# One rank for each operation in a fused set-attention and expert kernel: a new fixed order, a second pass over the PSUM banks, and a reworked start

## The chip, the cores and the metric

The kernel runs on one core of a Trainium2 chip. Five engines work side by side: TensorE (PE in the profile, its weight loads PEld), VectorE (DVE), ScalarE (ACT), GpSimd (POOL), and SyncE (SP), which here only issues DMAs. The metric is the device time of one execution in microseconds (us); the median of several runs is compared.

## The reference, cut to what matters

```
x [4, 12480, 128], inducing I [32, 128], w_in [128, 2048], w_out [2048, 128]
mab(q, kv): s = q @ kv.T / sqrt(128); a = softmax(s); return a @ kv
h   = mab(I, x)                 # 32 rows for each of the 4 batches: the summary
y   = mab(x, h)                 # 49920 rows of 128
g   = relu-like(y @ w_in):  h >= 1: h;  h <= -1: 0;  between: (h + 1)^2 / 4
out = g @ w_out
```

The weights arrive as 8-byte floats and are turned into 4-byte floats on the chip, in pieces of 256 columns.

## The kernel before, in words

A batch is cut into 25 chunks of rows (15 of 512, 10 of 480), and the chunks into seven groups of up to four. For each batch `summarize` makes the summary `h`: the chunks of x are loaded (`xn`) and turned (`xT`), scored against `I`, exponentiated with the group's own maximum (`score`), turned back and multiplied with x (`gather`), which leaves one 128x128 piece `hs[:, g]` and one sum per group. A chain of small steps, `c1` to `c12`, then finds the common maximum, rescales the seven pieces by factors `ff` and adds them up by 14 matmuls in PSUM (`c11`: seven products in two instructions each). `attend` takes the second attention of a group, and its result `aT` is spread by DMA. Since `h @ w_in` is multiplied out once per batch (`multiply`, `spread` into `hw`), the hidden layer of a chunk is one product of `aT` and `hw`.

`chunk(b, c)` does the expert layer: for each of eight steps `k` there are two hidden tiles of 128 rows. Each is a matmul into one of seven PSUM banks (pool `h`; the eighth bank collects the output); `rise` (ScalarE) makes relu(h + 1) from the bank into `w`, `square` (ScalarE) squares both tiles in place, and `bound` (VectorE) takes min(w, max(h, 1)), reading the bank again, after which the bank is free. In six of eight steps `w` is then split into an upper part `hi` (on VectorE, ScalarE or GpSimd) and the rest `lo` (GpSimd), and three matmuls per tile are added to the output, otherwise two passes of full precision.

The two tiles of a step can lie in neighbouring banks. Then one `rise` or one `bound` reads both banks at once; else there are two instructions. The profile shows the joined form as 128x1024 (or 128x960), the single one as 128x512 (or 128x480).

The order of all instructions is fixed before the launch. Every operation is entered by `add` with its engine, cost, lag and a due time; `Plan.order` is a small list scheduler that steps through time, takes for each free engine the ready operation with the lowest due time, and gives out buffers (`Slot`s of the pools in `SLOTS`) as it goes. Due times come from the table `DUE` and, for some 850 operations, from a correction in `SHIFT`. Bank numbers are chosen as an operation is placed (`pick`), near the twin's bank where that is free, and two twins are joined only if they lie next to each other then. The resulting list is emitted as it stands, so each engine works through a fixed queue.

At the start the first batch's x, the weights and the masks are all prepared at once. w_out is loaded through buffers of the pools `w`, `hi` and `lo`, which 16 of batch 0's 25 chunks of x use too (`FIRST`). Matmuls on the identity (`keep_on`, L1184) fill TensorE's gaps from 14 us on.

Of the kernel before, what the change touches and what calls it, by code (L numbers as in the profile page):

```python
# [27 lines left out]
STEP = 1950  # L28

# [5 lines left out]
DUE = {  # L35
# [17 lines left out]
    "end": [-203620],  # L53
# [15 lines left out]
}  # L69

# [100 lines left out]
    },  # L171
}

WARM = (14000, 200)

LONE = {"r": 7750, "t": 3200}

KEEP = 100

WAIT = 175250  # L180

# [3 lines left out]
R = (18, 0.4167)  # L185


class Slot:


    def __init__(self, pool, turn=None, near=None):
        self.pool, self.left, self.until, self.place, self.tile = pool, 0, 0, None, None
        self.turn, self.near, self.pair = turn, near, near is not None
        if near:
            near.pair = True
# [1044 lines left out]
```

## Time and profile before

| | |
|---|---|
| median of 3 runs | 1708.54 us (1708.45 to 1711.73) |
| the profiled execution | span 1712.0 us |
| busy: TensorE / VectorE / ScalarE / GpSimd | 1690.1 / 1633.7 / 1638.5 / 1621.4 us |
| first hidden matmul | 64.69 us after the start of the span |
| moved by DMA | 105.66 MB |

The profiled execution is one execution taken by the hardware profiler, 3.5 us above the median of the runs. A span in which an engine works on an instruction counts as busy; instructions of one engine can overlap a little, and matmul records overlap a lot.

### The profile page before, as it was taken

Reading aid. Unit: us, or ns where it says so; the run is one execution under the profiler, and the core shown is the slowest. Engines: PE = TensorE matmul, PEld = TensorE weight load, DVE = VectorE, ACT = ScalarE, POOL = GpSimd, SP = SyncE. Lnnn points to the kernel's source line nnn. Section 1 sums busy time; section 2 is a strip of 40 time slices with the busy share of each in tenths; the row PEclk is TensorE's granted clock in tenths of the full one; section 3 lists DMA queues with packets and bytes.
Section 4 is the critical chain, followed back from the end, with each engine's and each line's share of the span. In section 5 each row is a group of like instructions: output and inputs, shape, how many; then the busy total and the mean of one; then the engine's idle time right before and its main releaser. Section 6 shows DMA issues by size and latency. Waiting matters only on the chain.

```text
span 1712.0 us, 25022 instructions
## 1 busy us (share of the span) xinstructions
PE 1690.1 (99%) x7716; PEld 1192.6 (70%) x7716; DVE 1633.7 (95%) x2119; ACT 1638.5 (96%) x2380; POOL 1621.4 (95%) x856
## 2 busy tenths in 40 slices
PE   7999999999999999999999999999999999999998
PEld 5756766677766667677776676667777766667776
DVE  5799999999899999999999999999999999999997
ACT  6699999999999999999999999999999999999997
POOL 2599999999999999999999999999999999999998
PEclk9899999999999999999999999999999999999999
DMA  9334433332343233333243333322212111111111
GB/s 275 87 54 81 79 61 65 54 75 50 66 79 74 48 72 66 59 59 70 50 96 54 74 66 69 60 56 55 41 31 58 30 33 36 28 36 36 33 32 18
DMA packets 427095, 105.66 MB, mean 62 GB/s; under 512 B 369842, under 2 KB 412434, under 8 KB 426962
## 3 DMA queue, kind: packets, MB, share of 16 engines
q1 hardware_dynamic: 425874, 103.82, 30.0%
q8 instruction: 61, 1.00, 0.3%
q14 instruction: 72, 0.59, 0.1%
q10 hardware_dynamic: 1088, 0.25, 0.1%
HBM read 48.94 MB, written 25.56 MB: 44 GB/s over the span
## 4 chain that ended last, share of the span: by engine, by line
PE 87%; DVE 6%; ACT 4%; issue 1%; DMA 1%; POOL 0%; SPq 0%; DVEq 0%; ACTq 0%; POOLq 0%
PE banks L1155 61%; PE banks L1083 19%; DVE w L1096 3%; ACT w L1091 2%; ACT w L1077 2%; DVE hi L1122 1%; PE banks L741 1%; PE banks L682 1%; PE banks L896 1%; PE banks L1184 1%; PE banks L725 1%; DMA w<-in_moe_w_out 1%; PE banks L639 1%; DVE oT L1167 1%; PE banks L824 0%
## 5 line engine op out<-in xcount | busy, mean ns | idle before, releaser
L1127 POOL TENSOR_TENSOR lo<-w,hi 128x1024 fp32r<-128x1024 f32 (+1 forms) x599 | 1394.1, 2360 | 20.4 <-PE banks L1155 5.2
L1096 DVE SCALAR_TENSOR_TENSOR w<-banks,w 128x512 f32<-128x512 f32 (+3 forms) x1159 | 953.2, 861 | 22.9 <-ACT w L1077 19.6
L1091 ACT ACTIVATE w<-banks 128x512 f32<-128x512 f32 (+3 forms) x1312 | 832.4, 704 | 22.7 <-PE banks L1083 20.1
L1077 ACT ACTIVATE w<-w 128x1024 f32<-128x1024 f32 (+1 forms) x800 | 826.9, 1068 | 3.1
L1083 PE MATMUL banks<-aT,hw 128*128 128x512 f32 (+1 forms) x1600 | 574.4, 429 | 3.0 <-DVE w L1096 2.1
L1155 PE MATMUL banks<-hi,w_lo 128*128 128x512 f32 (+1 forms) x1198 | 489.5, 409 | 2.9 <-DVE oT L1167 1.5
L1122 DVE TENSOR_REDUCE hi<-w 128x1024 fp32r<-128x1024 f32 (+1 forms) x406 | 474.0, 1176 | 10.8 <-PE banks L1155 1.5
L1155 PE MATMUL banks<-hi,w_hi 128*128 128x512 f32 (+1 forms) x1198 | 464.8, 388 | 0.0
L1155 PE MATMUL banks<-lo,w_hi 128*128 128x512 f32 (+1 forms) x1198 | 410.5, 428 | 0.1
L1083 PEld LDWEIGHTS banks<-aT,hw 128*128 128x128 f32 x1600 | 294.4, 188 | 151.5 <-DVE w L1096 58.8
L1155 PE MATMUL banks<-w,w_f 128*128 128x512 f32 (+1 forms) x804 | 392.1, 582 | 0.0
L1155 PEld LDWEIGHTS banks<-lo,w_hi 128*128 128x128 f32 x1198 | 222.8, 188 | 104.4 <-issue 52.5
L1155 PEld LDWEIGHTS banks<-hi,w_lo 128*128 128x128 f32 x1198 | 225.3, 188 | 83.6 <-issue 17.7
L1155 PEld LDWEIGHTS banks<-hi,w_hi 128*128 128x128 f32 x1198 | 225.5, 188 | 48.9 <-issue 9.9
L1155 PEld LDWEIGHTS banks<-w,w_f 128*128 128x128 f32 x804 | 151.0, 189 | 61.2 <-issue 37.8
L1116 POOL TENSOR_SCALAR hi<-w 128x1024 fp32r<-128x1024 f32 (+1 forms) x145 | 150.1, 1039 | 5.4 <-ACT s L916 0.8
L1167 DVE STREAM_TRANSPOSE oT<-banks 128x512 f32<-128x512 f32 (+1 forms) x100 | 69.3, 693 | 6.7 <-PE banks L1155 6.0
L660 DVE STREAM_TRANSPOSE xT<-xr 128x512 f32<-128x512 f32 (+1 forms) x75 | 50.7, 678 | 2.2 <-DMA xr<-in_x 2.2
L1120 ACT CAST hi<-w 128x1024 fp32r<-128x1024 f32 (+1 forms) x48 | 50.1, 1045 | 1.2 <-DVE w L1096 1.2
L939 POOL TENSOR_TENSOR a<-a,ahi 128x512 fp32r<-128x512 f32 (+3 forms) x28 | 35.7, 1276 | 2.1 <-ACT ahi L936 2.0
L568 POOL TENSOR_TENSOR w_in_sb<-aT,s 128x256 f32<-128x256 f32 x8 | 6.0, 752 | 31.9 <-DVE aT L557 31.9
L682 PE MATMUL banks<-xT,indT 128*32 128x512 f32 (+1 forms) x200 | 30.5, 612 | 0.0
(113 smaller groups left out, 574.6 us busy)
## 6 DMA issues: line engine op xcount, KB each, us to landing
out<-oT SPq DMA_DIRECT2D x240, 64.0 KB, 2.2
xn<-in_x SPq DMA_DIRECT2D x54, 256.0 KB, 4.1
xr<-in_x SPq DMA_DIRECT2D x180, 64.0 KB, 2.8
out<-oT SPq DMA_DIRECT2D x158, 60.0 KB, 2.2
aT<-ahi SPq DMA_DIRECT2D x118, 64.0 KB, 2.0
aT<-a SPq DMA_DIRECT2D x118, 64.0 KB, 2.0
xn<-in_x SPq DMA_DIRECT2D x30, 240.0 KB, 4.2
xr<-in_x SPq DMA_DIRECT2D x120, 60.0 KB, 2.6
```

Source lines behind the costliest of these rows:

```text
L660: nc.vector.transpose(make(xT[b, c])[:, : CW[c]], xr.tile[:, : NB[c]].rearrange("c n i -> c (n i)"))
L682: nc.tensor.matmul(p[q * M : (q + 1) * M, :cw], indT, xT[b, c].tile[:, :cw], start=True, stop=True)
L1077: nc.scalar.activation(w.tile[:, :, :cw], w.tile[:, :, :cw], AF.Square, scale=0.5)
L1083: nc.tensor.matmul(make(h)[:, :cw], hw[b][ft // 4].tile[:, ft % 4 * P : (ft % 4 + 1) * P], aT[b, c].tile[:, :cw], start=True, stop=True,)
L1091: each(of, i, hs_, lambda h, to: nc.scalar.activation(to, h, AF.Relu, bias=1.0), cw, w)
L1096: lambda h, t: nc.vector.scalar_tensor_tensor(t, h, 1.0, t, op0=ALU.max, op1=ALU.min), cw, w,
L1116: nc.gpsimd.tensor_scalar(make(hi)[:, :, :cw], w.tile[:, :, :cw], 1.0, 0.0, op0=ALU.mult, op1=ALU.add)
L1120: nc.scalar.copy(make(hi)[:, :, :cw], w.tile[:, :, :cw])
L1122: nc.vector.tensor_reduce(make(hi)[:, :, :cw], w.tile[:, :, :cw].unsqueeze(3), axis=AX.X, op=ALU.max)
L1127: nc.gpsimd.tensor_sub(make(lo)[:, :, :cw], w.tile[:, :, :cw], hi.tile[:, :, :cw].bitcast(F32))
L1155: nc.tensor.matmul(acc.tile[:, :cw], wt[k][:, i, :], g.tile[:, i, :cw], start=first, stop=(acc.parts == 0),)
L1167: nc.vector.transpose(make(oT)[:, :nb].rearrange("c n i -> c (n i)"), acc.tile[:, :cw])
```

## The change

- Each operation has its own rank in a list `ORDER` of 12093 numbers (the 250 identity matmuls have none, and come last), in place of `DUE`, `SHIFT`, `LONE`, `KEEP` and `WAIT`. The scheduler takes the ready operation of the lowest rank, and holds an engine for one of lower rank that becomes ready before the other would end.
- Where an operation can run on several engines, a string `ON` says on which (599 of its letters are for `hi`).
- Twins are joined whenever both are ready at once, wherever their banks are. After the order is made, `settle` gives out the bank numbers anew by a search that keeps up to 600 partial solutions and counts how many joined pairs are not neighbours; such a pair is issued as two instructions.
- The group sum moves from TensorE to VectorE: seven multiply-adds of 128x128 in `gathered`, then one matmul by `share`. `c3` also repeats the row of maxima, so that `c4` is one matmul.
- Start: the load of `inducing` goes out on ScalarE's DMA queue, and so do seven of batch 0's 16 `spread` transfers instead of two; the clear of `hs` and the masks move to GpSimd; the clamp of a weight block can run on GpSimd; w_out goes through `xr`, `hw` and `oT`; batch 1's loads may not start before 54 us; batch 0's exponentials use three buffers in turn; identity matmuls may start at 1.5 us; the first group's `attend` leaves out its first chunk, which `attend_first` has done.

```diff
-DUE = {
-    "h": [-67510, -9340, -84010, -9090, -128650, -5400, -235200, -125680],
...
-SHIFT = {
...
-WARM = (14000, 200)
-LONE = {"r": 7750, "t": 3200}
-KEEP = 100
-WAIT = 175250
+ORDER = [
...
+ON = (
...
+BEAM = 600
+WARM = (1500, 250)
...
+            choice = {e: w for e, w in choice.items() if e[0] == ON[self.chosen]}
...
+        rank = ORDER[n] if n < len(ORDER) and ORDER[n] >= 0 else 10**9 + n
...
-                    if op.merged and op.beside() and not (op.twin in able[e] and op.twin.ready(e) <= now):
-                        due += op.lone
-                    could.append((due, op.index, op))
+                    could.append((op.rank, op.index, op))
...
-                soon = min((at for due, at in coming if due + WAIT < best[0]), default=math.inf)
+                soon = min((at for rank, at in coming if rank < best[0]), default=math.inf)
...
-                        s.place = s.pick(spare[s.pool], now)
+                        s.place, s.begin = min(i for t, i in spare[s.pool] if t <= now), now
...
-                if best.merged and best.beside():
+                if best.merged and best.placed():
...
+                        x, y = best.uses[0], other.uses[0]
+                        x.mate, y.mate, x.joins, y.joins = y, x, x.joins + 1, y.joins + 1
...
+def settle(done, pool):
+    slots = sorted(dict.fromkeys(s for op in done for s in op.uses if s.pool == pool), key=lambda s: s.begin)
+    ways = [(0, (None,) * SLOTS[pool], None)]
+    for s in slots:
+        found = {}
+        for cost, held, past in ways:
+            held = tuple(x if x and x.until > s.begin else None for x in held)
+            for i, x in enumerate(held):
+                if x:
+                    continue
+                apart = s.mate in held and abs(held.index(s.mate) - i) != 1 if s.mate else False
+                way = cost + s.joins * apart, held[:i] + (s,) + held[i + 1 :], (i, past)
+                if way[1] not in found or way[0] < found[way[1]][0]:
+                    found[way[1]] = way
+        ways = heapq.nsmallest(BEAM, found.values(), key=lambda w: w[0])
+    past = ways[0][2]
+    for s in reversed(slots):
+        s.place, past = past
...
-        nc.vector.memset(hs, 0.0)
-        nc.vector.memset(m, 0.0)
+        nc.gpsimd.memset(m, 0.0)
...
-    ind_in = add("SP", 620, 2000, 100 * EARLY, lambda: nc.sync.dma_start(ind_sb, inducing))
-    masked = add("DVE", 900, 1050, EARLY + 2, masks, [folded], [mask])
+    ind_in = add("ACT", 640, 3000, lambda: nc.scalar.dma_start(ind_sb, inducing), span=(700, math.inf))
+    cleared = add("POOL", 900, 1050, lambda: nc.gpsimd.memset(hs, 0.0))
+    masked = add("POOL", 2400, 2550, masks, [folded], [mask])
...
+        v = single = add(dict(DVE=(268, 400), POOL=(420, 550)), 0, 0, to_single, [v], [home])
...
-        made, f = load_f32(src, when, due, after=got_all[0, 16])
+        made, f, value = load_f32(src, pools=("xr" if k % 2 else "hw", "oT", "oT"))
...
+        later = (54000 if b == 1 else 700, math.inf)
...
-            p1, e1[g] = Slot("h"), Slot("e1")
+            p1, e1[g] = Slot("h"), in_turn("e1") if b or g % 3 == 0 else Slot(["hx", "hy"][g % 3 - 1])
...
-                nc.tensor.matmul(p[:, :M], hs[:, g, :], ff[:, g, :], start=(g == 0), stop=(g == NG - 1))
+        def c10():
+            nc.scalar.activation(share, fold[:, 0, :], AF.Copy, scale=rs)
+        def gathered(groups):
+            a = s_a.tile or make(s_a)
+            for g in groups:
+                to, by = whole if g == NG - 1 else a[:, :C], fr[:, g : g + 1]
+                if g == 0:
+                    nc.vector.tensor_scalar(to, hs[:, g, :], by, None, op0=ALU.mult)
+                else:
+                    nc.vector.scalar_tensor_tensor(to, hs[:, g, :], by, a[:, :C], op0=ALU.mult, op1=ALU.add)
+        def c11():
+            nc.tensor.matmul(make(s_h)[:, :M], whole, share, start=True, stop=True)
...
-        cs = GROUPS[g]
+        cs = GROUPS[g] if b or g else GROUPS[g][1:]
...
-        if of[i].wide:
-            a, b = sorted(h.place for h in hs_)
+        a, b = sorted(h.place for h in hs_)
+        if of[i].wide and b - a == 1:
             do(banks[:, a : b + 1, :cw], *(w.tile[:, :, :cw] for w in ws))
+            return
+        for j in (0, 1) if of[i].wide else (i,):
+            do(hs_[j].tile[:, :cw], *(w.tile[:, half(j, hs_), :cw] for w in ws))
...
     done = plan.order()
+    settle(done, "h")
```

## Rows read from the trace of the kernel before

**Rows 1.** The page's engine shares: busy us, share of the span, instructions.

```profile
PE 1690.1 (99%) x7716; PEld 1192.6 (70%) x7716; DVE 1633.7 (95%) x2119; ACT 1638.5 (96%) x2380; POOL 1621.4 (95%) x856
```

**Rows 2.** Windows by stage: length, busy PE, PEld, DVE, ACT, POOL, clock, DMA share, GB/s.

```profile
0.00:64.69 64.69, 54.25 (x534) 39.36 (x534) 39.52 (x123) 34.44 (x83) 14.53 (x25) 0.92 0.69 209
64.69:1400.00 1335.31, 1330.43 (x5978) 935.11 (x5979) 1294.70 (x1639) 1305.87 (x1880) 1304.92 (x682) 1.00 0.32 62
1400.00:1700.00 300.00, 298.91 (x1186) 214.27 (x1184) 297.51 (x356) 297.77 (x419) 297.58 (x149) 1.00 0.17 32
```

**Rows 3.** The chain that ended last, first 125 us: start us, us, what.

```profile
30.76 5.62 DMA w<-in_moe_w_out
...
42.15 4.73 DMA w<-in_moe_w_out
...
51.47 3.13 PE banks L824 x14
...
64.69 1.12 PE banks L1083 x4
```

**Rows 4.** Order of time: DMA issues of SP, and TensorE's last transposes of x.

```profile
31.43 0.33 SPq L630 DMA_DIRECT2D w<-in_x  x1
34.34 5.05 SPq L630 DMA_DIRECT2D xn<-in_x  x7
...
39.85 0.63 PE L639 MATMUL banks<-ident,w 96*128 96x96 f32 x5
```

**Rows 5.** Windows of the start; the last number is GB/s.

```profile
10.00:20.00 10.00, 9.18 (x49) 6.34 (x47) 6.04 (x16) 6.05 (x12) 2.75 (x4) 1.00 1.05 352
30.00:40.00 10.00, 9.50 (x119) 5.77 (x118) 6.13 (x16) 9.03 (x25) 3.65 (x5) 1.00 1.01 282
```

**Rows 6.** Groups by line: busy us, mean ns | idle us before, releasers.

```profile
L1083 PEld LDWEIGHTS banks<-aT,hw 128*128 128x128 f32 x1600 | 294.4, 188 | 151.5 <-DVE w L1096 58.8 <-issue 29.3 <-DVE banks L902 2.6
...
L1096 DVE SCALAR_TENSOR_TENSOR w<-banks,w 128x512 f32<-128x512 f32 (+3 forms) x1159 | 953.2, 861 | 22.9 <-ACT w L1077 19.6 <-issue 0.2
L1091 ACT ACTIVATE w<-banks 128x512 f32<-128x512 f32 (+3 forms) x1312 | 832.4, 704 | 22.7 <-PE banks L1083 20.1 <-issue 0.2
...
L1122 DVE TENSOR_REDUCE hi<-w 128x1024 fp32r<-128x1024 f32 (+1 forms) x406 | 474.0, 1176 | 10.8 <-PE banks L1155 1.5 <-POOL lo L1127 0.4
...
L1116 POOL TENSOR_SCALAR hi<-w 128x1024 fp32r<-128x1024 f32 (+1 forms) x145 | 150.1, 1039 | 5.4 <-ACT s L916 0.8 <-DVE w L1096 0.7 <-PE banks L1083 0.6
...
L1120 ACT CAST hi<-w 128x1024 fp32r<-128x1024 f32 (+1 forms) x48 | 50.1, 1045 | 1.2 <-DVE w L1096 1.2
...
L824 PE MATMUL banks<-ff,hs 128*128 128x32 f32 x56 | 8.6, 302 | 0.0
```

**Rows 7.** The same view, shapes apart: single and joined, 512-column chunks.

```profile
L1091 ACT ACTIVATE w<-banks 128x512 f32<-128x512 f32 x636 | 357.5, 625 | 11.6 <-PE banks L1083 10.6 <-issue 0.2
...
L1096 DVE SCALAR_TENSOR_TENSOR w<-banks,w 128x1024 f32<-128x1024 f32 x249 | 297.8, 1211 | 9.3 <-ACT w L1077 8.7
...
L1096 DVE SCALAR_TENSOR_TENSOR w<-banks,w 128x512 f32<-128x512 f32 x462 | 292.8, 676 | 3.4 <-ACT w L1077 2.3 <-issue 0.2
...
L1091 ACT ACTIVATE w<-banks 128x1024 f32<-128x1024 f32 x162 | 167.3, 1047 | 0.0
```

**Rows 8.** One line's instructions, a w_out step: ns min/median/max, first to last start.

```profile
L557 DVE SCALAR_TENSOR_TENSOR hi<-w,hi x8: 402/418/426, 29.4 to 72.4; 128x256 f32<-128x256 uint32 x8
```

**Rows 9.** Order of time on VectorE at the start: a step of 128x128.

```profile
57.22 0.28 DVE L1002 TENSOR_TENSOR s<-banks,mx_first 128x128 f32<-128x128 f32 x1
```

**Rows 10.** Order of time on ScalarE: start us, us, merged instructions.

```profile
918.45 1.12 ACT L1091 ACTIVATE w<-banks 128x512 f32<-128x512 f32 x2
919.41 1.11 ACT L1077 ACTIVATE w<-w 128x1024 f32<-128x1024 f32 x1
...
922.00 1.93 ACT L1091 ACTIVATE w<-banks 128x1024 f32<-128x1024 f32 x2
923.81 1.06 ACT L1077 ACTIVATE w<-w 128x1024 f32<-128x1024 f32 x1
```

More of the change, by code (lines that the diff above doesn't have):

```diff
@@ L1 @@
+import heapq
 import math
@@ L408, in o_cols, with took @@
         return out[b * N + OFF[c] : b * N + OFF[c] + CW[c]].rearrange("(i n) c -> i n c", i=M)
-    def begins(b, c):
-        return (b * N + OFF[c]) * NP * STEP // 480
     def cost(c, fixed, each):
         return round(fixed + each * CW[c])
+    def took(w, fixed, each):
+        return round(fixed + each * w)
     FORM = dict(
@@ L506, in attn_moe, with load_f32 @@
     WS = 2 * P
[L508 to L510 removed]
+    def load_f32(src, dst=None, after=None, pools=("w", "hi", "lo")):
+        raw, home = Slot(pools[0]), Slot(pools[1])
+        other = home if pools[1] == pools[2] else Slot(pools[2])
+        mag, top = {}, {}
         rows = src.shape[1]
@@ L520, in take @@
                     nc.vector.tensor_copy(dst, raw.tile.rearrange("p (a b) -> p a b", a=dst.shape[1]))
-            f = add("SP", 700, 3000, when, fetch, [after], [raw])
-            return add("DVE", 205, 335, due, take, [f], [raw]), raw
+                mag[0] = raw.tile
+            f = add("SP", 700, 3000, fetch, [after], [raw])
+            return add("DVE", 205, 335, take, [f], [raw]), raw, mag
         def fetch():
@@ L576, in load_f32 @@
-        v = add("DVE", 420, 550, due, lower, [v], [raw, mag])
+                add_to(dst, by(mag[0]), by(t))
+        f = add("SP", 680, 3000, fetch, [after], [raw], span=(700, math.inf))
+        v = add("ACT", 290, 430, rebias, [f], [home, raw])
+        v = single = add(dict(DVE=(268, 400), POOL=(420, 550)), 0, 0, to_single, [v], [home])
+        v = add("DVE", 270, 400, shift, [v], [home, other])
+        v = add("DVE", 418, 550, upper, [v], [raw, other])
+        v = add("DVE", 263, 395, weight, [v], [home, other])
@@ L577, in load_f32, with load_in @@
+        v = add("DVE", 420, 550, lower, [v], [raw, home])
         both = 345 if dst is None else 470
-        joined = add(dict(DVE=(both, both + 130, due), POOL=(700, 850, due)), 0, 0, 0, join, [v], [mag, top])
-        return joined, mag
+        joined = add(dict(DVE=(both, both + 130), POOL=(700, 850)), 0, 0, join, [v], [home, other])
+        return joined, home, mag
     w_hi, w_lo, w_f, w_made = {}, {}, {}, {}
     in_made = []
-    def load_in(j, when, due):
+    def load_in(j):
         js = slice(j * WS, (j + 1) * WS)
@@ L778, in summarize @@
         rs = small("rs", [P, 1], f"_{b}")
-        ff = small("ff", [P, NG, M], "")
-        s_m, s_b, s_f, s_t, s_h = (Slot("h") for _ in range(5))
+        fr = small("fr", [P, NG], f"_{b}")
+        whole = small("whole", [P, C], "")
+        share = small("share", [P, M], "")
+        s_m, s_b, s_t, s_a, s_h = (Slot("h") for _ in range(5))
         def c1():
@@ L789, in c3 @@
             nc.vector.tensor_reduce(
-                mrow, s_m.tile[:1, :P].rearrange("o (q m) -> o m q", q=Q), axis=AX.X, op=ALU.max
+                mrow[:, :M], s_m.tile[:1, :P].rearrange("o (q m) -> o m q", q=Q), axis=AX.X, op=ALU.max
+            )
+            nc.vector.tensor_copy(
+                mrow[:, M:].rearrange("o (q m) -> o q m", m=M), mrow[:, :M].unsqueeze(1).to_broadcast([1, Q - 1, M])
             )
         def c4():
-            p = make(s_b)
-            for q in range(Q):
-                nc.tensor.matmul(p[q * M : (q + 1) * M, :1], mrow, one, start=True, stop=True)
+            nc.tensor.matmul(make(s_b)[:, :1], mrow, one, start=True, stop=True)
         def c5():
@@ L956, in attend @@
-        o = add("POOL", cost(n, 40, 2.41), cost(n, 145, 2.41), AT[10], lower, [o], [a, a_hi])
+        n = cw
+        o = state["attend"] = add("PE", took(n, 10, 1.75), took(n, 210, 1.75), scores, [hT_made[b], state["attend"], *(xT_made[b, c] for c in cs)],
+                [p2, s2, *(xT[b, c] for c in cs)], tiled=True)
+        o = add("DVE", took(n, 66, 1.11), took(n, 206, 1.11), turn, [o], [p2, p3])
+        o = add("DVE", took(n, 66, 1.04), took(n, 206, 1.04), most, [o], [p3])
+        o = add("DVE", took(n, 70, 1.04), took(n, 210, 1.04), less, [o], [s2, p3])
@@ L1025, in upper @@
         def upper():
-            nc.scalar.copy(make(t), p4.tile)
+            nc.scalar.copy(make(t)[:, :cw], p4.tile[:, :cw])
         def lower():
             half = slice(2 * M, 4 * M)
-            nc.vector.tensor_sub(t.tile[half], p4.tile[half], t.tile[half].bitcast(F32))
-        o = add("PE", 240, 440, 3 * EARLY, scores, [hT_made[0], xT_made[0, 0]], [p2, p3, s2, xT[0, 0]], tiled=True)
-        o = add("DVE", 225, 365, 3 * EARLY, turn, [o], [p2, p3])
-        o = add("DVE", 200, 340, 3 * EARLY, most, [o], [p3])
@@ L1043, in attend_first @@
-        o = add("DVE", 560, 700, 3 * EARLY, lower, [o], [t, p4])
+            nc.vector.tensor_sub(t.tile[half, :cw], p4.tile[half, :cw], t.tile[half, :cw].bitcast(F32))
+        o = add("PE", 240, 440, scores, [hT_made[0], xT_made[0, 0]], [p2, p3, s2, xT[0, 0]], tiled=True)
+        o = add("DVE", took(W, 66, 1.11), took(W, 206, 1.11), turn, [o], [p2, p3])
+        o = add("DVE", took(W, 66, 1.04), took(W, 206, 1.04), most, [o], [p3])
+        o = add("DVE", took(W, 70, 1.04), took(W, 210, 1.04), less, [o], [s2, p3])
@@ L1044, in attend_first @@
+        o = add("DVE", took(cw, 66, 1.05), took(cw, 206, 1.05), lower, [o], [t, p4])
         aT_made[0, 0] = [o]
```

396 lines of the change are left out of this document (181 added, 215 removed), and 728 rows, old and new, of tables (DUE, ORDER, SHIFT).

## The prediction

> **What bounds the kernel now.** I read the page's engine shares first [rows 1], then the windows by stage [rows 2], the chain of waits at the start [rows 3], and the groups of instructions [rows 6]. No engine stands out: VectorE, ScalarE and GpSimd are each busy for 95 to 96% of the span. TensorE shows 99%, but its records overlap, and in the packed part it often waits: 58.8 us of weight loads for hidden matmuls wait for a `bound` (L1096) to give a bank back [rows 6]. Since all four share the work, I keep one account for each of the other three: work, idle before the first hidden matmul (64.69, rows 2 and 3), idle in the packed stretch 64.69 to 1700, and idle in the last 12 us. The last 12 us are what is left of the totals [rows 1]. Each line adds up to the span of 1712.0:
>
> - ScalarE 1638.5 + 30.3 + 31.7 + 11.6
> - VectorE 1633.7 + 25.2 + 43.1 + 10.0
> - GpSimd 1621.4 + 50.2 + 32.8 + 7.6
>
> Between 1400 and 1700 ScalarE is idle for 2.2 us of 300, or 0.7%; from 64.69 to 1400 for 29.4 of 1335, or 2.2%. So the packed stretch can be fuller than it mostly is. The profiled execution's 1712.0 is 3.5 us above the median of the runs (1708.5); I make the sum against 1712.0 and take 3.5 off at the end.
>
> **The start.** Before, w_out is loaded through the buffers `w`, `hi` and `lo` that the first x tiles need, and its loads stand among x's. The chain of waits shows the price: 5.62 and 4.73 us on w_out transfers [rows 3], behind which ScalarE's queue (exponentials and copies of the summary) stands. SP issues the last x load of batch 0 at 31.43, and seven loads of batch 1 from 34.34 on compete with what is left [rows 4]. After the change w_out goes through `xr`, `hw` and `oT`, the 25 x tiles find 25 free buffers, and batch 1 is held back to 54 us. Before the last x tile then lie 25 x tiles and 7 of the 8 w_in blocks, 8.2 MB by their sizes. At the 352 and 282 GB/s of two saturated windows [rows 5] that is 23 to 29 us, so with 2 us before the first bytes the last tile is there at 25 to 31, where SP had only issued it at 31.43.
>
> From the last tile to the first hidden matmul the old chain took about 25 us (its transposes began at 39.85, rows 4). Out of it go most of the second w_out wait, about 2.5 us on ScalarE; the 14 matmuls of the group sum, 3.13 us [rows 3], against one matmul and one last VectorE step of 0.28 [rows 9]; and about 1.5 us of matmuls that ran at a low clock there. That leaves 18. First hidden matmul: 28 + 2 + 18, about 49 instead of 64.7, with 45 and 56 as ends (fast transfers; or one more wait like the 5.62, since ScalarE still converts w_out blocks 0 and 1 ahead of the last exponentials in the new list).
>
> The 15.7 us don't all come off the end, since work moves from the idle start into the packed stretch. In ORDER, five of the eight w_out first steps and three of the nine w_out copies on ScalarE stand ahead of the first hidden matmul; before, nearly all did. At about 0.42 each (by the nearest row, rows 8) 3.4 us move, and ScalarE's 34.4 busy us in the start become 31 of 49: idle 18, **-12**. VectorE keeps about 31 (some fifteen steps of w_out of about 0.4 [rows 8] move later, masks and clears leave, the group sum comes): idle 18, **-7**. GpSimd gains masks, clears and clamps and loses five late joins: about 18 of 49, idle 31, **-19**. Moving the load of `inducing` to ScalarE's queue spares SP one issue of about 0.4 us; the saturated windows hide it, and if they don't it is that 0.4.
>
> **Work on each engine.** Counted in the lists of the diff:
>
> - `hi` (three engines can make it): 386 VectorE, 151 GpSimd, 62 ScalarE, against 406, 145, 48 [rows 6]. Mean durations are 1.18, 1.04 and 1.05; instructions of one engine overlap a little, so I take 1.12, 1.0 and 0.96: VectorE -22.5, GpSimd +6, ScalarE +13.5 (bounds by the means: -23.5, +6.2, +14.6).
> - Joined tiles: the two `rise` of a pair stand next to each other in ORDER in 383 of 800 pairs and the two `bound` in 597. Before, 1312 and 1159 instructions did 1600 tiles [rows 6], so 288 and 441 were joined. By busy time over count [rows 7], two singles cost 1.124 and a joined one 1.033 on ScalarE, 1.268 and 1.196 on VectorE: 0.09 and 0.07 each. But those durations overlap. In the order of time [rows 10] two singles started at 918.45 and the next instruction at 919.41, 0.96 later, and two joined ones took 1.81 from 922.00, 0.905 each: 0.055 on ScalarE. I take that, and 0.05 for VectorE: -5.2 for 95 more joins and -8 for 156 (bounds: nothing if no bank neighbours are found, -8.6 and -11).
> - Group sum: 28 steps of 128x128 on VectorE at the 0.28 of the nearest row [rows 9], +8, and four scalings on ScalarE, about +0.5 with the saved copies.
> - Clamps: 12 of 16 go to GpSimd: -4 and +5 at most (0.42 by L557, rows 8, for either, a little more on GpSimd). Masks and clears -2 and +3; two joins return to VectorE.
>
> The group sum is where the two ways of reading TensorE part. Its 56 matmuls were 8.6 us of busy time [rows 6] on the engine that shows 99% [rows 1], so by the busy column it earns 8.6. The Trainium skill (Perfetto Trace Analysis, Identifying the Most-Contended Engine) calls matmul busy time a poor measure and wants the busy share of weight loads, here 70% [rows 1]; by it TensorE has room, the 8.6 earn nothing, and 8 us land on an engine at 95%. I follow the waits of L1083's weight loads, which say the same, and count only the 3 us of the start.
>
> The skill also has a price for a join (the same page, Optimizing Scalar/DVE Operations): a fixed access cost of about 51 ns for ScalarE and 125 ns for VectorE on PSUM. By the first the 95 joins earn 4.8, which agrees with 5.2; by the second 156 joins would earn 19.5 instead of 8, an estimate by that page that the busy time over count contradicts (0.07 at most).
>
> Sum of the work: ScalarE +9, VectorE -28, GpSimd +12.5. With the packed idle as before: ScalarE 1712 + 9 - 12 = 1709; GpSimd 1712 + 12.5 - 19 = 1705.5; VectorE 1712 - 28 - 7 = 1677. So ScalarE ends last, and VectorE has some 30 us to spare.
>
> **What the spare VectorE time is worth.** ScalarE's largest packed wait is `rise` for hidden matmuls, 20.1 us, and these in turn wait for VectorE's `bound` to free a bank [rows 6]. An engine with about 72 us idle instead of 43 takes a `bound` sooner. The trace can't price this; the ends are nothing, and the 0.7% of the last 300 us for the whole stretch, 12 us instead of 31.7, -20. I take the middle, half of the 20.1 and a little, -11: 1698, less 3.5, **1695**.
>
> **Rivals.** A change below 0.2% (3.4 us) I count as none, which is about what runs of this kernel can tell.
>
> *Only the start improves.* The fixed order still runs into the same waits, and ScalarE keeps 31.7 of idle: 1709 - 3.5 = 1705, on the border between faster and same. For it: ScalarE gets more work and is the last engine. Against: its wait hangs on the engine that is relieved. Chance 0.20.
>
> *The packed stretch becomes as full as the last 300 us.* 1709 - 20 - 3.5 = 1685. For it: that stretch exists in this trace, at the same work for each tile; against: it has no summary and no transposes of a next batch in between. Chance 0.20.
>
> *Banks run short: slower.* A joined instruction holds both banks until its end. The first bank of a pair is kept 0.56 longer on VectorE (1.196 against 0.634) and 0.47 on ScalarE [rows 7]: 156 x 0.56 + 95 x 0.47 = 132 us of one bank, 19 us for all seven `h` banks, on a TensorE that already waits 58.8 for them. If two thirds reach ScalarE's packed idle, 1709 + 13 - 3.5 = 1718. It decides once `rise` waits over 24 us (20.1 + 4) for hidden matmuls. Against: joining was chosen in the order only where both tiles are ready at once, so the second bank often waits anyway. Chance 0.12.
>
> *The second pass finds no neighbouring banks for the additional pairs.* Each is then issued as two instructions, and the joins earn nothing: 1695 + 5 = 1700. Seven banks and up to 597 pairs speak for some of it; pairs are spread over the run, so most should fit. Chance 0.08.
>
> **How the numbers follow.** The forecast has 0.40 and its own range is 1689 to 1702 (the start 4 us earlier or later, packed idle 6 us either way). Range 1680 to 1709: it takes in the first two rivals and the fourth with the start's ends, and leaves out the bank rival and the earliest corner of the second, together about 0.18. Faster is the forecast, the second and fourth rival and half of the first: 0.78. Same is the other half of the first: 0.10. Slower is the bank rival: 0.12.
>
> **What would show it.** First hidden matmul near 49 in the chain of waits, with no w_out transfer above 3 us in it; about 380 joined `rise` and close to 600 joined `bound`; VectorE near 1606 busy, ScalarE near 1647, GpSimd near 1634; ScalarE's wait of `rise` for hidden matmuls near 10 us. The forecast is wrong if the first hidden matmul comes after 56, if that wait doesn't fall, or if joined instructions come out near 288 and 441.

## The result: 1.0% slower, and the profile after

| | before | after |
|---|---|---|
| median | 1710.13 us (1708.45 to 1713.67, 4 runs) | 1727.84 us (1725.86 to 1728.84, 4 runs) |
| ratio | 1 | 1.0100, 95% interval 1.0085 to 1.0115 |
| span of the profiled execution | 1712.0 us | 1726.3 us |

The forecast was 1695, with 1709 as its upper end.

The page's engine shares of the kernel after answer to [rows 1]:

```profile
PE 1704.5 (99%) x7726; PEld 1185.8 (69%) x7726; DVE 1633.5 (95%) x2002; ACT 1665.1 (96%) x2322; POOL 1633.4 (95%) x878
```

The same windows as [rows 2]:

```profile
0.00:64.69 64.69, 59.14 (x625) 46.85 (x626) 43.24 (x120) 40.81 (x92) 22.86 (x43) 1.00 0.69 202
64.69:1400.00 1335.31, 1325.46 (x5851) 913.67 (x5850) 1278.81 (x1544) 1311.38 (x1811) 1296.52 (x679) 1.00 0.32 62
1400.00:1700.00 300.00, 298.93 (x1175) 210.57 (x1173) 295.47 (x324) 298.28 (x404) 295.98 (x149) 1.00 0.17 32
```

The first 64.69 us hold more work than before (ScalarE +6.4, VectorE +3.7, GpSimd +8.3), and yet the end is later: it is the packed stretch that got longer. The chain that ended last, from the first hidden matmul (L1580) to the first projection (L1652):

```profile
54.93 1.14 PE banks L1580 x4
...
67.37 1.20 DVE oT L1032
68.59 3.58 DVE oT L1038
72.19 0.44 DVE oT L1043
...
73.00 1.29 DVE w L1593 x2
74.33 1.09 PE banks L1580 x3
75.42 1.60 PE banks L1652 x5
```

The first hidden matmul comes at 54.9 instead of 64.7 [rows 3]. The matmul of the first projection starts at 75.26 where it started at 75.28 before (the chain's 75.42 is where the piece ahead of it ends): the ten microseconds are used up. Over half of them, from 67.4 to 73.0, go into steps on the last w_out block that stand in front of the `bound`s (`w L1593`). The groups that answer to [rows 6, 7], first by line, then ScalarE's `rise` with shapes apart:

```profile
L1593 DVE SCALAR_TENSOR_TENSOR w<-banks,w 128x1024 f32<-128x1024 f32 (+3 forms) x1048 | 948.9, 940 | 42.5 <-ACT w L1574 30.6
L1588 ACT ACTIVATE w<-banks 128x512 f32<-128x512 f32 (+3 forms) x1239 | 816.6, 712 | 14.2 <-PE banks L1580 9.0
...
L1580 PEld LDWEIGHTS banks<-aT,hw 128*128 128x128 f32 x1600 | 293.4, 188 | 156.9 <-DVE w L1593 58.9
```

```profile
L1588 ACT ACTIVATE w<-banks 128x512 f32<-128x512 f32 x562 | 311.7, 604 | 5.8 <-PE banks L1580 3.6
L1588 ACT ACTIVATE w<-banks 128x1024 f32<-128x1024 f32 x199 | 203.1, 1030 | 1.7 <-PE banks L1580 1.3
```

361 pairs of `rise` and 552 of `bound` are joined (288 and 441 before; the new order pairs 380 and 596, so the second pass left 63 apart). ScalarE's wait for hidden matmuls fell from 20.1 to 9.0. None of the three signs that were to show the forecast wrong is there, and yet the time went the other way. Of the signs that were to show it right, two busy times are missing: ScalarE was to be near 1647 and is at 1665.1, VectorE near 1606 and is at 1633.5 (GpSimd is where it was forecast, 1633.4 for 1634).

**Holes in TensorE's stream.** The experiments below turn on one number worked out from the starts in the trace. Go through TensorE's operations in order, and let each take what the kernel's scheduler books for it: 231 ns for a matmul of 512 columns, 218 for 480, 860 and 806 for the two passes of `w` with `w_f`. The starts in a full stretch do follow one another so (0.22 us for 480 columns). Where an operation starts over 0.04 us later than that, the delay is a hole, and the booking goes on from its start. Between 76 and 1690 us the holes sum to 26.7 us before (212 of them) and 44.6 after (351). That is 17.9 more; the span grew by 14.3; and by the same costs TensorE lost about 5 us of work to the moved group sum in that stretch (three sums of 1.6). By the engine on which the last of what the late operation needs came to its end, holes behind VectorE grew from about 20 to 30, behind GpSimd from 4 to 9. But in 10.4 of the 26.7 and in 23.6 of the 44.6 all of it had ended more than half a microsecond earlier, so there the trace shows no such wait. Two kinds of these can be told apart. 3.2 us after, and none before, are matmuls at a lower granted clock (two stretches of 3.4 us, from 75.9 and from 1284.2). And 9.5 us after, 4.4 before, stand right behind a matmul whose own weight load came late; the last section shows one.

### The profile page after: what moved, and what is told of

The parts are those of the page before. It is cut to its first block, busy times and chain, and to the rows that moved or that the text cites. A ratio compares the mean times of both kernels' runs of the same rounds, so it can differ in the third digit from the quotient of the medians.

```text
span 1726.3 us, 24950 instructions
## 1 busy us (share of the span) xinstructions
PE 1704.5 (99%) x7726; PEld 1185.8 (69%) x7726; DVE 1633.5 (95%) x2002; ACT 1665.1 (96%) x2322; POOL 1633.4 (95%) x878
## 4 chain that ended last, share of the span: by engine, by line
PE 89%; ACT 4%; DVE 4%; issue 1%; POOL 1%; DMA 1%; DVEq 0%; ACTq 0%; SPq 0%; POOLq 0%
PE banks L1652 63%; PE banks L1580 20%; ACT w L1588 2%; DVE w L1593 2%; ACT w L1574 1%; PE banks L1394 1%; PE banks L1229 1%; PE banks L1168 1%; PE banks L1680 1%; POOL lo L1624 1%; DVE hi L1619 1%; PE banks L1210 1%; DVE oT L1664 1%; PE banks L1126 0%; DMA hw<-in_moe_w_in 0%
## 5 line engine op out<-in xcount | busy, mean ns | idle before, releaser
L1593 DVE SCALAR_TENSOR_TENSOR w<-banks,w 128x1024 f32<-128x1024 f32 (+3 forms) x1048 | 948.9, 940 | 42.5 <-ACT w L1574 30.6
L1588 ACT ACTIVATE w<-banks 128x512 f32<-128x512 f32 (+3 forms) x1239 | 816.6, 712 | 14.2 <-PE banks L1580 9.0
L1574 ACT ACTIVATE w<-w 128x1024 f32<-128x1024 f32 (+1 forms) x800 | 817.1, 1048 | 7.2
L1580 PE MATMUL banks<-aT,hw 128*128 128x512 f32 (+1 forms) x1600 | 540.7, 422 | 5.5 <-DVE w L1593 4.7
L1652 PE MATMUL banks<-hi,w_lo 128*128 128x512 f32 (+1 forms) x1198 | 518.3, 433 | 1.3 <-DVE oT L1664 0.8
L1652 PE MATMUL banks<-hi,w_hi 128*128 128x512 f32 (+1 forms) x1198 | 466.8, 390 | 0.0
L1652 PE MATMUL banks<-lo,w_hi 128*128 128x512 f32 (+1 forms) x1198 | 458.3, 433 | 1.7 <-DVE oT L1664 1.5
L1619 DVE TENSOR_REDUCE hi<-w 128x1024 fp32r<-128x1024 f32 (+1 forms) x386 | 451.7, 1179 | 8.0 <-PE banks L1652 0.8
L1580 PEld LDWEIGHTS banks<-aT,hw 128*128 128x128 f32 x1600 | 293.4, 188 | 156.9 <-DVE w L1593 58.9
L1652 PE MATMUL banks<-w,w_f 128*128 128x512 f32 (+1 forms) x804 | 397.2, 583 | 0.0
L1652 PEld LDWEIGHTS banks<-hi,w_lo 128*128 128x128 f32 x1198 | 225.4, 188 | 103.1 <-issue 39.0
L1652 PEld LDWEIGHTS banks<-lo,w_hi 128*128 128x128 f32 x1198 | 222.5, 188 | 106.1 <-issue 47.0
L1652 PEld LDWEIGHTS banks<-hi,w_hi 128*128 128x128 f32 x1198 | 225.8, 188 | 62.4 <-issue 25.3
L1652 PEld LDWEIGHTS banks<-w,w_f 128*128 128x128 f32 x804 | 150.9, 189 | 48.9 <-issue 21.8
L1617 ACT CAST hi<-w 128x1024 fp32r<-128x1024 f32 (+1 forms) x62 | 63.4, 1025 | 0.0
L1680 PE MATMUL banks<-ident 128*128 128x128 f32 x208 | 28.5, 288 | 2.1 <-POOL ident masks.py:199 2.1
L1680 PEld LDWEIGHTS banks<-ident 128*128 128x128 f32 x208 | 26.6, 201 | 5.0 <-issue 2.7
```

Of the source, the lines that this page charges most:

```text
L1574: nc.scalar.activation(w.tile[:, :, :cw], w.tile[:, :, :cw], AF.Square, scale=0.5)
L1580: nc.tensor.matmul(make(h)[:, :cw], hw[b][ft // 4].tile[:, ft % 4 * P : (ft % 4 + 1) * P], aT[b, c].tile[:, :cw], start=True, stop=True,)
L1588: each(of, i, hs_, lambda h, to: nc.scalar.activation(to, h, AF.Relu, bias=1.0), cw, w)
L1593: lambda h, t: nc.vector.scalar_tensor_tensor(t, h, 1.0, t, op0=ALU.max, op1=ALU.min), cw, w,
L1617: nc.scalar.copy(make(hi)[:, :, :cw], w.tile[:, :, :cw])
L1619: nc.vector.tensor_reduce(make(hi)[:, :, :cw], w.tile[:, :, :cw].unsqueeze(3), axis=AX.X, op=ALU.max)
```

## The experiments

Each was timed in five rounds against the kernel before; a ratio is to be held against the 1.0100 of the kernel after. Edits are to the kernel after unless said otherwise. Span and holes are of the profiled execution.

| run | ratio, 95% interval | span | holes |
|---|---|---|---|
| before / after | 1 / 1.0100 | 1712.0 / 1726.3 | 26.7 / 44.6 |
| 20 `hi` from GpSimd to VectorE | 1.0214 (1.0196 to 1.0232) | 1743.4 | 61.5 |
| 20 `hi` from ScalarE to VectorE | 1.0193 (1.0172 to 1.0213) | 1737.6 | 58.2 |
| squares parted from their rise | 1.0292 (1.0275 to 1.0310) | 1761.0 | 77.6 |
| no joins | 1.0195 (1.0176 to 1.0213) | 1742.1 | 58.9 |
| group sum on TensorE | 1.0183 (1.0165 to 1.0201) | 1740.0 | 57.4 |
| less VectorE / GpSimd / ScalarE | 1.0096 / 1.0090 / 1.0092 (each 0.0015 or 0.0016 either way) | 1726.3 / 1726.2 / 1722.2 | 44.0 / 43.9 / 41.6 |
| less of all three | 1.0092 (1.0078 to 1.0105) | 1722.4 | 40.6 |
| less TensorE | 1.0092 (1.0078 to 1.0106) | 1722.5 | - |
| less of all four | 1.0062 (1.0048 to 1.0076) | 1716.6 | - |
| before, 20 `hi` from GpSimd to VectorE | 1.0104 (1.0090 to 1.0117) | 1727.6 | 42.2 |
| product from PSUM | 1.0086 (1.0073 to 1.0099) | 1721.9 | 39.8 |
| two late steps left out | 1.0090 (1.0076 to 1.0104) | 1726.1 | 43.6 |
| both | 1.0079 (1.0067 to 1.0091) | 1723.2 | 41.0 |
| before, products from SBUF | 1.0035 (1.0022 to 1.0048) | 1719.5 | 33.2 |
| before, more TensorE | 1.0087 (1.0073 to 1.0101) | 1723.8 | - |
| no second pass | 1.0163 (1.0149 to 1.0177) | 1734.1 | 52.9 |

(Where TensorE's own matmuls are left out or doubled, holes can't be compared.) In every other run the span's distance from 1712.0 is that of the holes from 26.7, to within 1.0 us in the two variants of the kernel before and 1.9 to 5.9 us less in those of the kernel after. This is bookkeeping and no cause: TensorE does the same work in all these runs, so whatever makes one longer appears as holes in its stream.

### Which engine is too full?

Theory A: the new order puts 226 squares directly behind the `rise` that they read (97 before), and ScalarE stands still each time. Theory B: GpSimd's work grew and sets the time. Theory C: a joined operation holds two banks until both halves are there.

```diff
     settle(done, "h")
+    mine = [op for op in done if op.engine == "POOL" and ... ["hi", "w"]]   # second run: "ACT"
+    for op in mine[3 :: len(mine) // 20][:20]:
+        op.engine = "DVE"
...
+    done = parted(done)      # third run: such a square and ScalarE's next operation change places
...
-        if of[i].wide and b - a == 1:      # fourth run: never joined
+        if False and of[i].wide and b - a == 1:
```

> The kernel after, with 20 of its 151 copies hi of GpSimd given to VectorE at the same places of the order. Theory A (the new order puts squares directly behind the rise that they read, and ScalarE stands still each time): GpSimd is only followed, so 1724 to 1731 us. Theory B (GpSimd is the fullest engine, its work at back-to-back pace grew by 14.5 us and the time followed it): 20 x 1.03 = 20.6 us less for GpSimd, so 1708 to 1716 us, where ScalarE takes over. VectorE gets 20 x 1.10 = 22 us, which it has spare under both.

> The kernel after, with 20 of its 62 copies hi of ScalarE given to VectorE at the same places of the order. Theory A: ScalarE sets the pace, and gets 20 x 0.94 = 18.8 us back: 1710 to 1718 us. Theory B: GpSimd's work is as before, so 1724 to 1730 us.

> The kernel after, where a square that stands directly behind its own rise on ScalarE changes places with ScalarE's next operation if nothing between forbids it: 111 such squares stay of 226 (the kernel before has 97). No work is added or moved to another engine. Theory A: 115 x 0.17 us = 20 us of standing still go from ScalarE, so 1710 to 1718 us. Theory B: 1725 to 1730 us.

> The kernel after, where every rise and every bound is issued for one bank, none for two; the order stays. By the single and joined rows that is 361 x 0.05 = 18 us more for ScalarE and 552 x 0.064 = 35 us more for VectorE. If the joins pay what their rows say and ScalarE sets the pace (theory A): 1740 to 1750 us. If GpSimd sets it (theory B): 1726 to 1734 us. Theory C (joined operations hold two banks until both halves are there, and that is what made the kernel slower): 1712 to 1724 us.

All four were slower than the kernel after by 0.9 to 1.9%. The first three lie above what A and B forecast; the fourth, 1744.6, lies in A's range of 1740 to 1750. In the first two runs what was taken from one engine was given to VectorE: together, 20.6 us less on GpSimd or 18.8 less on ScalarE and 22 more on VectorE cost 16 to 19. They can't tell a relief that is worth nothing from one that VectorE's load covers up; the runs further down, which only take work away, can. In the third run the squares directly behind their rise fell from 226 to 111, and ScalarE was busy as long as in the kernel after (1665.5 us for 1665.1) and stood idle longer, so in its own test theory A failed. The third run's waits (engine, line, releaser: us, times, longest), where L1612 is `hidden`, L1625 `bound`, L1606 `square`, L1620 `rise`:

```profile
PEld banks L1612 <- DVE w L1625: 89.6, 203, 3.8
DVE w L1625 <- ACT w L1606: 65.0, 125, 2.3
...
ACT w L1620 <- PE banks L1612: 30.4, 77, 2.0
```

In the kernel after these read 58.9, 30.6 and 9.0. These rows suggest that a later square makes its `bound` later, that this keeps a bank, and that TensorE waits. Without joins the time is 0.95% longer: joins may hold banks, but they save more than that costs, so theory C does not explain the loss.

### Is the group sum the cost?

```diff
+            if 0 in groups:
+                nc.vector.tensor_tensor(ff, fr..., fold..., op=ALU.mult)
             for g in groups:
-                nc.vector.scalar_tensor_tensor(to, hs[:, g, :], by, a[:, :C], ...)
+                nc.tensor.matmul(a[:M, :C], ff[:, g, :], hs[:, g, :], start=(g == 0), stop=(g == NG - 1))
```

> The kernel after in its own order, with the multiply-adds of the group sum done by TensorE again (one product of VectorE makes the weights, seven matmuls, one copy), at the places of the order where VectorE did them. VectorE gets back some 1.9 us in a row per batch. Theory G (the jumps at the batch changes, 3.1 us near 860 us and 3.4 us near 1280 us, are the six multiply-adds in a row on VectorE): 1718 to 1723 us. Rival (the jumps come from the order around them, and the sum only stands there): 1725 to 1731 us.

0.8% slower than the kernel after, outside both. Its new product took up to 2.4 us where it alone needs 0.37:

```profile
L1312 DVE TENSOR_TENSOR ff<-fr,fold x4: 374/1164/2415, 43.6 to 1297.7; 128x224 f32<-128x224 f32 x4
```

Seven matmuls stand behind it in TensorE's queue, and behind them everything else. So this run says nothing against the group sum on VectorE, but it pointed to the products (below).

### Is relief of any engine worth anything?

Part of the work is left out, so the outputs of these runs lack it.

```diff
+    for op in mine[3 :: len(mine) // 40][:40]:
+        op.light = True
...
-                nc.scalar.activation(w.tile[:, :, :cw], w.tile[:, :, :cw], AF.Square, scale=0.5)
+                nc.scalar.activation(w.tile[:, :part, :cw], w.tile[:, :part, :cw], AF.Square, scale=0.5)
```

(likewise `bound` for one bank of a joined pair, `lo` for one half, and single matmuls skipped)

> The kernel after, with 40 of its joined bounds made over the first bank alone (the other half stays without its bound): 40 x 0.53 = 21 us less for VectorE, spread over the run, nothing else changed. If VectorE sets the time: 1706 to 1712 us. If no engine alone does and the engines wait for each other in turn: 1716 to 1724 us. If another engine sets it: 1726 to 1730 us.

> The kernel after, with 18 of its lo operations of GpSimd made over the first half alone (the matmuls read that half for both): 18 x 1.18 = 21 us less for GpSimd, spread over the run. If GpSimd sets the time (its work is the largest of the three): 1706 to 1712 us. If the engines wait for each other in turn: 1716 to 1724 us. If another engine sets it: 1726 to 1730 us.

> The kernel after, with 40 of its 800 squares made over the first half alone (the other half is not squared): 40 x 0.47 = 19 us less for ScalarE, spread over the run. If ScalarE sets the time: 1708 to 1714 us. If the engines wait for each other in turn: 1716 to 1724 us. If another engine sets it: 1726 to 1730 us.

> The kernel after with the three lightenings together: 40 joined bounds over one bank alone (21 us of VectorE), 18 lo over one half (21 us of GpSimd), 40 squares over one half (19 us of ScalarE). Each alone gave 0 to 2 us. Theory C (the three engines are equally full in this order, so each takes over where another is relieved): 1707 to 1715 us. Theory P (TensorE's stream, whose busy row reads 99%, sets the time): 1723 to 1728 us. Theory L (waits along the chain of a tile set it, whatever the loads): 1715 to 1723 us.

> The kernel after, with 90 of the 4398 matmuls of the projection left out (90 of the products of w_lo with hi): 90 x 0.23 = 21 us less for TensorE, spread over the run, nothing else changed. Theory P (TensorE's stream sets the time): 1706 to 1712 us. Theories C and L (it waits for the others): 1724 to 1729 us.

> The kernel after with all four lightenings together (21 us of VectorE, 21 of GpSimd, 19 of ScalarE, 21 of TensorE). Theory C: as with three, 1706 to 1714 us. Theory P: 1704 to 1711 us. Theory L: 1714 to 1722 us. If all four are equally full: three alone give little and four give some 19 us, 1706 to 1711 us.

(Of the 90 operations chosen on TensorE 85 lost a matmul, 19 us: the first product of a sum is never skipped.) No relief of one engine shows: 1.0090 to 1.0096 against 1.0100, each inside the other's interval. Nor does that of three together. Only with all four does the time fall, by 0.0038 x 1709 = 6.5 us of some 20. So no theory held that names one engine (B, P), nor C in its form with three engines. "All four equally full" is not confirmed either: it forecast 1706 to 1711 for four, and the time is 1718.9. Theory L, that waits along the chain of a tile set the time whatever the loads, came nearest: 1724.7 and 1718.9 lie in its ranges, and 1724.4 for three engines is 1.4 us above. Which waits these are, no run isolates.

The same move in the kernel before:

```diff
+    mine = [op for op in done if op.engine == "POOL" and op.start > 60000 and ...]
+    for op in mine[3 :: len(mine) // 20][:20]:
+        op.engine = "DVE"
```

> The kernel before, in its own order, with 20 of its 145 copies hi of GpSimd given to VectorE: the same move that cost the kernel after 19 us. If the kernel before keeps room in its order (its VectorE has 82 us of excess over its back-to-back pace between 100 and 1700 us, the kernel after 117): 1711 to 1718 us. If every order of this kind pays a move in full: 1727 to 1732 us.

It cost 1.04%, 18 us, for 22 us more on VectorE and 20 less on GpSimd: the order of the kernel before has no more room for this move than the new one. What was put in was paid in both kernels; what was taken out, which was tried in the kernel after alone, was mostly not returned.

### VectorE's products that wait for GpSimd

In order of time near the last batch change of the kernel after, all three engines:

```profile
1276.16 6.67 POOL L1624 TENSOR_TENSOR lo<-w,hi 128x960 fp32r<-128x960 f32 x3
...
1280.73 2.12 DVE L1295 TENSOR_TENSOR fs<-fr,sg 128x7 f32<-128x7 f32 x1 [0.31 <-ACT fr L1292]
...
1282.89 0.16 DVE L1296 TENSOR_REDUCE tot<-fs 128x1 f32<-128x7 f32 x1
...
1283.19 0.35 PE L1299 MATMUL banks<-tot,fold 128*128 128x1 f32 x2 [1.47 <-DVE tot L1296]
...
1284.85 0.60 PE L1652 MATMUL banks<-hi,w_lo 128*128 128x480 f32 x1
```

A product of seven columns lasts 2.12 us, and ends where GpSimd's `lo` ends (1276.16 + 6.67 = 1282.83). Before, the exponentials lay in PSUM and the four products took 0.13 to 0.17. At the start the bit operations of the late w_out block show the same, 0.28 alone:

```profile
68.25 1.45 POOL L1437 TENSOR_TENSOR a<-a,ahi 96x512 fp32r<-96x512 f32 x1
...
68.59 3.56 DVE L1038 TENSOR_SCALAR oT<-oT 128x256 uint32<-128x256 uint32 x1
...
69.65 2.36 POOL L1624 TENSOR_TENSOR lo<-w,hi 128x1024 fp32r<-128x1024 f32 x1
```

The Trainium skill (SBUF — State Buffer, section SBUF: two separate sides) says that GpSimd and VectorE share one pair of ports as an exclusive lock, taken by VectorE in its two-port mode or, against a GpSimd operation that reads SBUF, with two inputs in SBUF, and that the loser waits for the whole instruction. The trace agrees for the product: 2.12 us until GpSimd's end, at most 0.17 where one input was in PSUM. The 3.56 us last until the end of two GpSimd operations in a row; that this step, with one input, runs in the two-port mode is not shown here.

```diff
+            two = (s_t.tile or make(s_t))[:, 256 : 256 + NG]
+            nc.scalar.activation(two, mg, AF.Exp, bias=nm, scale=SCALE)
             nc.scalar.activation(fr, mg, AF.Exp, bias=nm, scale=SCALE)
...
-            nc.vector.tensor_mul(fs, fr, sg)
+            nc.vector.tensor_mul(fs, s_t.tile[:, 256 : 256 + NG], sg)
...
     def upper():  /  def weight():      # second run, the last w_out block alone
+            if last:
+                return
...
-            nc.scalar.activation(make(s_f)[:, :NG], mg, AF.Exp, bias=nm, scale=SCALE)   # kernel before
+            nc.scalar.activation(fr, mg, AF.Exp, bias=nm, scale=SCALE)
```

> The kernel after, where the product fs at each batch change reads the exponentials from PSUM, as in the kernel before (ScalarE writes them there too, one operation of 0.3 us more per batch). Theory W (VectorE's products with both inputs in SBUF wait until GpSimd's running operation ends, 1.2 and 1.7 us at the last two batch changes, TensorE's stream waits behind them, and it is paid in full): 3 to 6 us less, ratio 1.0065 to 1.0085. Rival (the jumps at the batch changes have another cause): ratio 1.0095 to 1.0110.

> The kernel after, with two bit operations on the last block of w_out left out (the ones that lasted 1.20 and 3.57 us near 68 us; the block's values are then wrong). Theory W: 3 to 5 us less, ratio 1.0070 to 1.0085. Rival (the first tiles wait for something else anyway, and the lead of the start is used up by then): ratio 1.0092 to 1.0105.

> The kernel after with both changes of the two runs before. Theory W: 6 to 10 us less, ratio 1.0040 to 1.0065. Rival: above 1.0090.

> The kernel before, with the exponentials of each batch change written to SBUF instead of PSUM, so that two products of VectorE per batch read SBUF alone. Theory W: each waits 0 to 2.2 us for the running lo, six of them beside a full stream, and TensorE waits behind them: 3 to 8 us more, ratio 1.0020 to 1.0050. Rival: 0.9990 to 1.0015.

From PSUM the product takes 0.16 again, and the time falls by 0.0014 x 1710 = 2.4 us (the profiled span by 4.4): just short of theory W (VectorE's products wait for GpSimd's running operation, and that is paid), and not clear of the kernel after, whose interval begins at 1.0085. Some 1.7 of the 4.4 go with the low clock from 75.9 on, which this execution does not have there, and which the product does not explain. In the kernel before the placement costs 0.35%, 6 us, clear of noise and as W said; there a second product of each batch, `ff`, reads SBUF alone too, and took up to 2.19 us where it took 0.45. The second run is a miss: with two operations gone the next two wait instead, now `lower` and `join`, as its chain shows:

```profile
69.10 1.20 DVE oT L1047
70.33 2.12 DVE oT L1055
```

So the wait at the start was not taken away, and what it costs stays open. Both together give 3.6 us of 17, less than the 6 to 10 that W forecast.

### Was TensorE full before? And the second pass alone

```diff
+                            if me[0].twice and wt is w_lo and not first and acc.parts:   # kernel before
+                                nc.tensor.matmul(acc.tile[:, :cw], ..., start=False, stop=False)
...
-    settle(done, "h")      # kernel after, second run
```

> The kernel before, with 90 of its 4398 matmuls of the projection issued twice (products of w_lo with hi, spread over the run, so those sums count one term double): 90 x 0.23 = 21 us more for TensorE, nothing for the other engines. Theory T (TensorE's stream is as good as full, and what is put into it or holds it up is paid): 15 to 21 us more, ratio 1.0088 to 1.0123. The prediction's reading (TensorE often waits and has room): ratio 0.9990 to 1.0030.

> The kernel after without the second pass: bank numbers as the first pass gives them, the order and the planned pairs unchanged. 137 rises and 201 bounds are then joined instead of 361 and 552; the other pairs are issued as two, 351 x 0.064 = 22 us more for VectorE, 224 x 0.05 = 11 us more for ScalarE. In proportion to the run without any join (913 pairs split cost 16 to 17 us) 575 pairs cost 10 us: ratio 1.0140 to 1.0180. If every such microsecond of VectorE is paid: above 1.0200. If the joins are worth nothing by themselves: 1.0090 to 1.0115.

Of the 90 operations chosen 83 got a second matmul (the first product of a sum is never doubled), so 19 us went in. They cost 0.87%, 15 us: TensorE had little room that this order could use, and the prediction's reading falls. By itself this doesn't make TensorE the engine that sets the time, since 22 us on VectorE cost as much. The waits of this run show why it misled; L1083 is `hidden`, as in [rows 6]:

```profile
PEld banks L1083 <- DVE w L1096: 39.4, 139, 0.8
...
ACT w L1091 <- PE banks L1083: 27.0, 58, 2.0
```

The wait of weight loads for `bound`, 58.8 before, shrank by 19.4 us, as if TensorE had used its spare time; the run became longer all the same, and ScalarE waits 27.0 for hidden matmuls instead of 20.1. A weight load mostly runs ahead of its matmul, under the one before, so most of its wait is no hole in the matmuls.

Without the second pass the time is 0.63% or 11 us longer: it earns that in this order, and the 63 pairs that it leaves apart are too few for the loss.

## Why the prediction was wrong, point by point

- **The sum.** It was ScalarE's account: 1712 + 9 of work - 12 at the start - 11 of packed idle = 1698. In the windows of [rows 2] ScalarE's busy time grew by 26.6 us, its idle time fell by 6.4 in the first 64.69 us and by 6.0 from there to 1700: 1712 + 26.6 - 6.4 - 6.0 = 1726.2, and 1726.3 was measured. So 17.6 of the 28.3 us that the sum was off by are in the term "work", 5.6 in the start and 5 in the packed idle.
- **First hidden matmul at 49 (45 to 56).** 54.9: inside, near the late end. **Start idle -12, -7, -19.** Off: by the first window the three engines did 6.4, 3.7 and 8.3 us more of their work in the first 64.69 us. The first projection did not come earlier (75.26 against 75.28); late w_out steps stand between the first hidden matmuls and it.
- **Work on each engine.** About right. At the pace at which like instructions follow one another back to back (the tenth percentile of start to start of each shape), ScalarE's work went from 1597 to 1603 us, VectorE's from 1575 to 1551, GpSimd's from 1619 to 1634: +6, -24, +15, where +9, -28, +12.5 were forecast. The joins came (361 and 552), and without any the kernel is 16 us slower. But busy time is not this work, and the accounts add up busy time. ScalarE's instructions lasted 46.5 us less in sum (1891.1 for 1937.6) and overlapped by 226.1 us instead of 299.1, which leaves the 26.6 more. A square directly behind the rise that it reads starts 0.03 us after that rise ends; behind another operation's rise it starts over 0.1 us before the end. There are 226 of the first kind instead of 97. That this alone took the overlap is not shown: with 111 of them ScalarE's busy time stayed.
- **"TensorE often waits", and one account for each of the other three.** This is the step that failed: it took an engine's busy time as given by its list of work, its idle time as room, and left TensorE out. It rested on the 58.8 us that weight loads wait. Matmuls put into the kernel before are paid at 15 us of 19, and the holes in TensorE's stream were 26.7 us of 1614, not 58.8 and more. The Trainium skill (Perfetto Trace Analysis, Identifying the Most-Contended Engine) says that matmul busy time is not a good measure of how near TensorE is to its limit, and names the busy share of weight loads as one to use instead; here its 70% pointed to room that was not there, and the 99% was nearer.
- **The packed idle falls by 11 because VectorE is relieved.** VectorE's work did fall by 24, and ScalarE's wait for hidden matmuls fell to 9.0 (forecast: near 10). But relief was worth next to nothing: 21 us more of it change nothing that can be measured, and neither do 20 on three engines at once. Instead the span was 175 us more than VectorE's back-to-back work (137 before), and VectorE's wait for squares rose from 19.6 to 30.6.
- **Group sum, TensorE's 8.6 us worth nothing but the start's 3.** The span grew by 3.6 us less than the holes, about the work that left TensorE's stream in the packed stretch. That it earned this is an account, not a run: the one run on it was spoilt by its product.
- **Rivals.** Banks run short, slower by another way: its sign did not come (`rise` waits 9.0, not 24), and without joins it is slower still. No neighbouring banks: 63 of 976 pairs. That the order itself fits the chip less well was not among the rivals. The kernel's scheduler books the start of the last output's transpose at 1692.0 before and 1694.0 after, so its own plan was not shorter; the chip came 14.6 and 27.0 us later than planned. For the first output it was 11.3 and 11.1: the kernel before loses 3 us to its plan over the whole packed stretch, the kernel after 16.

**What stays open.** Why the holes grew by 17.9 us is not shown. The product at the batch changes accounts for about 3 (44.6 to 39.8, without the low clock from 75.9 on). The rest are many short ones, 0.13 us on the mean, spread over the run; those right behind a late weight load grew by 5.1. Operations that stand directly behind their producer are more (226 squares for 97, and 204 `bound`s within 0.06 us of their square's end for 102), but parting the squares made it worse, so this as the cause is only argued. Exchanging the whole order of the packed stretch between the two kernels was not tried, since buffers are given out along with the order.

## What to carry to other kernels

Where four engines are at 95% or more in a fixed order, an account of one engine's work plus idle can miss the sign: busy time itself changes with the order. Before counting a relief as a gain, take some work away and see whether the time falls; adding work shows less, since here it was paid on each engine that got some. Read TensorE's load from the starts of its matmuls, not from waits of weight loads. When an operand moves from PSUM to SBUF, look whether VectorE's instruction now reads SBUF alone while GpSimd is busy.

## What the runs showed of the hardware that was not expected

A hole in TensorE's stream can be followed by a stretch at a lower clock, which costs as much again. In the kernel after TensorE stood 1.47 us at the batch change above, and the next four microseconds ran at a granted clock of 0.57 on the mean, 3.4 us of them at the lower of its two levels (1.2 GHz), 0.40 us for a matmul of 480 columns instead of 0.22. Windows as in [rows 2]:

```profile
1280.00:1284.00 4.00, 2.53 (x24) 1.88 (x24) 3.65 (x4) 2.31 (x5) 2.83 (x2) 1.00 0.02 2
1284.00:1288.00 4.00, 4.00 (x13) 3.32 (x12) 3.75 (x12) 2.81 (x4) 2.57 (x2) 0.57 0.00 0
1288.00:1292.00 4.00, 4.00 (x18) 2.88 (x16) 1.84 (x4) 3.71 (x6) 3.92 (x4) 1.00 0.00 0
```

That is 0.43 x 4 = 1.7 us more, behind a product of seven columns. With the product in PSUM the same windows stay at 1.00:

```profile
1280.00:1284.00 4.00, 4.00 (x21) 3.46 (x21) 3.43 (x11) 4.00 (x8) 2.99 (x3) 1.00 0.01 4
1284.00:1288.00 4.00, 4.00 (x16) 2.60 (x14) 3.37 (x7) 4.00 (x8) 4.00 (x3) 1.00 0.01 2
```

It doesn't always come: in the kernel after TensorE stood for 2.89 us up to 74.33, and from 75.9 on the granted clock was at the lower level for 3.4 us; in the run with the product in PSUM it stood for 2.87 us up to 74.87, and the clock stayed at 1.00.

A weight load that comes late costs more than its wait. Around 100 us of the kernel after one waited for a `bound` and began together with its matmul:

```profile
99.34 0.40 PE L1580 MATMUL banks<-aT,hw 128*128 128x512 f32 x1
...
100.50 0.19 PEld L1580 LDWEIGHTS banks<-aT,hw 128*128 128x128 f32 x1 [0.73 <-DVE w L1593]
100.50 0.50 PE L1580 MATMUL banks<-aT,hw 128*128 128x512 f32 x1
...
100.84 0.39 PE L1652 MATMUL banks<-hi,w_lo 128*128 128x512 f32 x1
...
101.06 0.40 PE L1652 MATMUL banks<-hi,w_hi 128*128 128x512 f32 x1
```

The next matmul starts 0.34 us later instead of 0.22 to 0.23. So it is for the 129 matmuls of 512 columns in this trace, between 80 and 1690 us, whose load began less than 0.02 us ahead of them: 0.337 us on the median to the next start, 0.234 for the others.
